# A new table of start slots and engine choices for a two-layer attention and feed-forward kernel

## The chip, the cores and the metric

The kernel runs on one core of one Trainium2 chip. The metric is the device time of one execution in microseconds (us), of which three runs of the kernel before are at hand. Engines are named as the profile names them: PE is the matrix engine, PEld its weight loads, DVE the vector engine, ACT the scalar engine, POOL GpSimd, and SP the engine that issues nearly all DMAs; SPq is SP's queue of DMA issues. The profile times one execution, instruction by instruction.

## The reference, cut to what matters

```python
x = A_x                                            # (1, 2048, 1024), bfloat16
x = x + _A_ref(_layernorm(x), A_wqkv, A_wo)        # attention, 32 heads of 32
x = x + _B_ref(_layernorm(x), B_w1, B_b1, B_w2, B_b2)
x = x + _A_ref(_layernorm(x), A_wqkv, A_wo)        # the same weights again
x = x + _B_ref(_layernorm(x), B_w1, B_b1, B_w2, B_b2)

# _A_ref: q, k, v = x @ wqkv; each token attends to W = 8 tokens, 2 apart (0, 2, ..., 14 back):
#   softmax(q . k * Dh**-0.5) over those 8, the sum of their v, then @ wo
# _B_ref: h = relu(x @ w1 + b1); (h * h) @ w2 + b2, with F = 3584
```

## The kernel before

The 2048 tokens are cut into four blocks of 512, and the two layers make eight units u = 0 to 7. A unit does layer norm and transpose of its block (SA), the q, k and v products (SQ, or SQ7 with seven block products in place of eight), the window attention on DVE (S2: products named P, sums named tree, weighted values named pr), the wo product with residual and second layer norm (SW), the first feed-forward product with its squared relu (SF1) and the second (SF2). From unit 1 on the feed-forward products, and from unit 3 on the q, k and v products, use the seven-product scheme: sums of weight blocks (tiles tv, made on DVE) are stored to DRAM once (w1s, wqs, tw) and loaded in later units like weights. Their results meet in PSUM banks X, Y and Z. A bank is drained either by ACT into a tile u or by DVE, in `hc` (line 1118, rr<-u,Y or rr<-u,Z) and `qc` (line 842); the relu and square of the feed-forward are `hr` (line 1125 on DVE, 1127 on ACT), `relu` (1166, 1169) and `sq` (1135, 1137).

Work of neighbouring units is interleaved. Weights come in tiles `w` of up to 1 MB (line 442, issued by SP; nine slots of class 8K). The layer-normed block is transposed by a DMA `lnT` (line 618, also on SP; its source is xn). In unit 0 the transposes are done on PE (pt, line 657) and drained by `ptc`.

Nothing in this order is found by the engines at run time. `Plan` builds a list of 4133 operations with their dependencies, and each engine gets its operations in one fixed order. That order, and which of two engines does an operation that may run on either, come from a table, `STARTS`:

```python
raw = zlib.decompress(base64.b85decode(STARTS))
n = len(raw) // 3
for i, o in enumerate(self.ops):
    o.num, o.prio, o.pick = i, raw[i] + 256 * raw[n + i], raw[2 * n + i]
    if o.pick:
        o.eng, o.dur, o.lat, o.fn = o.alt
```

So operation i has a start slot (16 bits, one slot is 0.02 us of the planner's own time) and one bit that picks its second engine. `run` then places the operations by these slots; sorting each engine's operations by slot gives the order in the program. The planner has its own constants for durations and transfers (a DMA lands a mean time after the queue has come to it); these are not in the table and do not change. Semaphores follow from the order: an instruction waits for what it reads, and for the last user of the buffer slot that it writes. A class of buffers hands out its slots in about the order in which their last users come in the program. Class 2K (eight slots) matters below: xt, xn, tv and rr share it, so an `hc` that opens a new rr can have to wait for the landing of a store of tv or of a transpose of xn.

Of the kernel before, what the change touches and what calls it, by code (L numbers as in the profile page):

```python
# [17 lines left out]
H = 32  # L18
W = 8
# [28 lines left out]
def _win_ap(a2d, col0, n, nw=W, wstep=-1):  # L48
# [5 lines left out]
    "c-rlF1z1(vwm)0x5Co;W6p-$cMkEvjq`SLA>F#b2rKAK2K}xzC0Rcfu6l@Hz<3HBMd*8X|o^$Sb@Bh8`?z`XptvSb-Bj%W6jJ@~TYj2DyT*Z{-<L`CdH|S+dx<2x|>r@|+O`dF>+WL5eRs5Xw<z6h#"  # L54
    "j7o={ug_hMTY2{MymF=rbSI+?$^9~9Pkw37TJ=tmOeywNEX`XQ^{N<0**_TIyHwykRQwu}@LBAIawYfjCt@}UR!nN%J0?oy4G(7C-W}SB^U^knn+xu;&mf$CR&`ZreXnWs3)%Qq(Q~{X=1#uZ@>i3u"
    "gne5)syX(o8@I3zwU4oWk5&lt#p!c%61OfZMpQ`Q-^3O<JnFN<x_3sfTr?ER<@<ojJGHQOQsb8aP2W8@MN@X9{NDt--#)!?vh%%THFxkVQ|MAaoh@D9JcgDxtN5)E+fnNw0vA%Bb~=jzBKO@3J<Oeq"
    "4ihb>NW2^-$b9p@4&%{dkdHVsp3h!T)#gi~YU(?EICf-zT;?2o)5sj2W@=|F{dpgzZ<b%=!|O<N-;K7XsJlM4$Y)oodvle<KYNf+(lE}iqJNE9;F+lU+r+zS_a)1+XwR`PXAd402pwI*p;a^Y*&XK5"
    "YAGzxZO_w4PU!IegeTUC;b|4$^!XD?oa6mN`!N+knuOKrw<EN9BM)9)e^enER9t*E5i`L<G|VbJtf6T71OK34`!s=a^?uIRZ|e#lFin%+)~;d-MLvnb#-XJd#HeNp(7sdDo?L%SQNq!@it)U>n_Iv!"
    "lX$F&)7PrEXlJM{?69|Bkc@n{s(r#R_x?imiO3bR*IgXsy5lSx0S((d=_B7&XGr6<beI`w9*)Tc*KYGyqzwMJSo~FPh$7{pf%5Ym#tgiO#yYlk7a^JsQdjTTXNSre4F^YVJ)cuFbB@m)Quc8!pwm$B"
    "3dtnLb!&e0&hw2!;TGBCw|6Xq^=E{9-cYd?()N=kch;<63NG)C$Q5~Mj7D8GOG)W+%!_SpjAiH_XYk+aU>39Mezi(OB>i-rDgV7{X*un*Yhlms_Hh=SZ=|32%~j8boX3<YJ)t-C_0%_=2$dz=yH^&Q"  # L60
    "A1{-C<Qo0>=tACoi>yP~F^A4wyJk3GZ;|!9^C`J}r7;)hXA_?#Zh^%Bje5;n6TDo{945Xzqqfe>?Ds55>oH3%7)Kf61mm21DiYLr$Z#&~!+elz%<!I4#;S|p;GSea<tLGil(-3UpXP_MYjTmQ%a(i@"
    "iQgZZh%-K>jd^-pDY$Qsg+KJXQ|;<AQDXJh+}bCrS%c4mPG_ZvNqMDXifqf<=JdW^CuU4++~hJ+y)-Nm!gq0tJ8IzDxU`>4+??J}`p8_-#z&IQ_ldM3VVH!eheiz>@HE%R)x!&iqs+Daze|#*yJk64"
    "jaQsC+zql><h_0Mz3km>r|w*{hc(Pz5>EwD7ZOMxq?D>rd3<qi?<21NuIw-0Pvl&ymoMiw@`_C{mr64D(2eJ3c4yQwQsOgm_nrD*I0X@98?4MITza>Clp<qwh9WR;ptsfa$83|&ZXs)2uU=86X(5NJ"
    "26fcB>}3Ld#|DwW<jTTj?~}B4ckn5cKD0{dr6w&tXJvXxxW($7yngiTg~=aGJ%=2znya#?UpJ8F_AKq^F5>C9-*c9`^xXY@i&Q`Bd9osdDB2C*`aM3EJc(O|_R6QcUx~A<oEUEq3`uI6_QXr;(&aMD"
    "ANz>kS@dFdN>u9k6Y7YN2AeY{EiyQ3*L`W!#y=~5RbeOU9oX9<^^Bm#o3_0WzDmfhnX@Q#ZZBb$^z>~mx!4UNuPE!6+{!u6zTURSkT>~AP}J~LKQ$aj&@?Nq=Rs7{m#KA%ZhU!On}_F!VjgRzd>ZoX"
    "Di$tEJSux_ozTnlbkh@)M_dKNl;>YwP^`YsXr8z#oA3QPeVjAA4uh~q%)MRpg>5&9W!k7!fn=p_=blXF1R-r7eGax<1i8~QPUqfF@933DM;yyMpB3VMR(pA65=)WC)*$T-XXNSLZVI;vtbn-<su6dI"
    "diFe)x^3FpVV=hGu_&`yt9Amca+fy-evd34?S4wpcOMukrSEf0<(W&xh^ybP?X`VC7~DeK^+mi(^djA8!>dCn2GexB_GI)L#mi2cQtym2>NixH%d|fV`_b7SHK@mme9>W0A`xUfrX2o+KVis1&;NSr"
    "Ol3R~0|}n0@letz_5Q3`X@vOop^caoBW$mC&Dz_29BVgiGD(E?-@2+c3RuqX5W1Vnh<<-Dy5;$VNj>$@kGFz-868K4Y}Q&GC7dYj+X$U}q>3dAqX)ZC$EtG3o?3cOI1*G;3}(ONl#jdFEA!=Oa7VeR"
    "sBhEWqv19z3Jy%iTP2Tvh+<<+Q_;J;Q0EPJ{~(qmHf3^1c91k-o7_C*3-{|P6RABc_aZIkMO2%s%IjP~&8@L3l8zZumv@4X9=GU!`-9iy@Sx{8NsH8wx<@<8(PK3C@icqrTzj9p@}Dp=2zf7J)%1na"
    "a8p!e&fsMNiAv3n1;NIcuGQm<W%(M+xUx>B*}ZM?>*5~G-`a7x=~Nas6cTqCY|9^;<XI1kTzxMc)QSH#eScd;t@;^-J%iM>Ej!(&Jtj}nj3<na#ZI~8&spTtkEzK#^l+)ce07EFZO_N7$sw~dm5PC$"  # L70
    "{rj};{V4^0DpW>q9A$7+JR6?s#9^<8<1030HMmz{NO+Ag$3IM?d9q-*OG;~)p-!W;RJ6>`c-xh}(s8>sXPMc4WUgfC%F(GvqLXc0%}nmYAG8Q4tF|xWzBKD-l4B2kX1K2S#npQPPpCrjCN-D!9kL&l"
    "0vgx#1udHfnIgT2ryrP`I_jiYKlW*-7Z?-H7`?fD(!wURQ@KoUP4_xy5}yivFs`%Ve)J||{O5)r+(y<ESj!LijIgh-|F9{;jT@Ap^lM_(p9vLQHLW!lS&+-OcrxIW*mqW{vt_gF;)|y{Vno^xIe10!"
    ">5p~nTM=WYW-L%y964%Y({RIQTaYEbL$@X!SIYa^((bNZ;p^0PvBzh*JZG423u_;}*X7BX+Q#0s4w~vJqu1LwYp~VC@j>zxgSXW6I{Mdj>ll1X@sDEWY}HYnD*=wp4O_WdpELJ{xMV7?OiX<7<-JUF"
    ")MSI0PQ8p!Uy^#NaB`Cb2j$=TNOg)Oe_14k^O#Y=h@`M|<S3CTS@>Ya9!25J?%7SM(v@b?)I0BN3U7Z;c&0Axv%f>nn<MLIUo;?|_prQvMc|oJMqC?)ex$u5Wwg`LetcD5&L39}dvm%^6H6AfP4=;r"
    "zJW)BBPE_MWR;s$d#ODp-*US4?>_QV37s25seGl=Wz^s2R%`LSU+fX2^<`S@QbR-;6}#m9Kr(}hFDyDA?gdq2TP}=XINV?|%zI;3<oIzzEaebWYUQj=MfX$wkp}-~^7e(wh5I}n!x7cZJ*|DqZ`XUe"
    "7Q^Z8Q?6K{{Aain+>S={Ea9t`+@&mhMf)&$n?<*pHvQSwh59cqE>L~bNlV-hU=`L=7K-N3m~FgoOV){#X8NrpB;=Jt`NE{#Gp>uYq;V7xFIdSVvgDmTBSqz^Nqn+P6t5_@wq#B|Nj~jM^zBY}l}Qe1"
    "hZb2MC%d5po9)X%RrOU?eLvLh&ZlKv%gvM4-w5){sx&LGX6Y!I19q3Si$qA=g2@{xh_J9_S9oG2jUBTE8qG3eMum!>?33MEiy7sY3+iFSt2`vHEky2X9V>Sm_k(!E<Ia7iKy$P4H!l4&!h`1vr81Aa"
    "aWa&e`EhMZwUXsJ!#T&>FA6Tr#nPZOg4)gw@n)I?41d5B^2>d6q>5BG%Daw5?cw!o?&|v@Hn+Jv$B6R`qzYCT-0>eNRLrxP2M-Ec-uh@UubJd|GBHr9Y-LY~{&N7E$u#z*M23XsinS8W*bzeQ-dVg2"
    "jmEc$68UYxo8P=h^l}!yT7`Y$O6G8{$2w24C^26n-NdR@LK3;dlbW)i>@~2nvP^26ajSVXrpuHNOPX&!K`?UPqT$F+{2uNV0`lj~BCa`~B@&Np@wATei=VQ-{i1YJmHb?Z;*I=_e#Tc?;}!)GB&v6g"
    "DF)qh=%JLUtabc^sgO^>mp)FguqkHexzqK*;N|7l#MJHqL@P4=79Jl&hr-u5+B^2NY$!v|jQdVuN@uy(w#yQI6YUzLO%U4Z5>k&^Raz*t#x}`!ZyMwYD^1U#aDF8xsB~uVjWq28H-9Q(W#0knvo|;_"  # L80
    "M$gMk&k<JceHU(?UC?uItX4st7&%px-YLz73eic_YiAapZRL;J622zOaYSQUNY&;_INe$Y(HE{%27cG=CL4>HqsBUdjYP+uW_+;IkV@*hVI>p(f>Whvlkh@n+c?>KA;V&3=U@SiD^n}xrBB!>QkJIt"
    "ReXZl2Yy6#;X3G_{i-Z<xywAIVVpadH}lifegmue2`@dis&^LjD^G>-CPFcIm3`yy2vJy_y{Qz@GydT7`;%!UyGa+lSR=dFj~rL(z%MQod+Bn8+eApqAz`GMTxo}b!|o=wT7yH}42kYX+Op?d0a#a>"
    "j0%V?MxC*ZG`HD5c-;IVz;5yhBmA^4nc9^P)5)oN$ueA4fe)5QY9HNtyVkrt-%Dn2!+7kIZ0OO5*Vt@_v1{H5nlF%=%{Pw>N(EMa`b3z3=kg<Y>WlhwqWYcI*KJ!zEvvU#SDqwMlN?cQxVoc%T*AZV"
    "N(UjQuT)hLj%z{c4^vO&-cbq1`g_a<&lbdUZ*E6)2sH0nIVuDS+3%qUW&CG!vnlS2xDT68Xgp#wyX~GD9Z);CnuXyzHH1TF{+hGsE9r?Bfk_zC)Q^{kE#@TIl=-SO)9l|z<#VY8zc_AP*lX6p{Z4z9"
    "g?htoZh0{_t(f(BGf|+zoX=#YlpBW8SCJv<cwEl=^HdsAkIyOvQEORLm^3|)>$z*HAGRdy5=qsBFYhLPWBc5-b@E<<PiEQM^E&tBw#zX;C`3%Zm}4&6J>hf*&!F_Mtz$rM=`7Br79yEYuH;#~sH*)f"
    "%5TDF3~HwIZ6Y+8d$ZP0Tnt_m#5i+uMEmnv<RH5#PFR0r6Tv2r4VJnhN8J&|u^8Ssmo8(CY@a^DResOqCzQ_RjnB#wUp`_n3a@yay?{DJoTkH1zgD?OZ`$G0T^389`i|M5>WNNCn?M;uc+(fjkXe$&"
    "?-mvK8Ozj0*h+7Ni{6k3NavsHA~D_}wQn*>HL7^`_H?{;MtEo6J{{A&Cg)b=6KdxVKg{1|UAtuYiR7k|b3x&9WvI~UaSETZ;+duGdAHbTxrB#D#e-GrT~b53wRml<iwDz59@9yB8K#NN)Z1PieMQ*0"
    "#}IjLxBf}{n<vs*NvFqrzmeHAWKB8LD8`kKlFQ}Xdw%K^CTR+}1(l{xbD4A5$Oqi0-W4+6{M9!sFWK0%2C?K7%@s3dHoi{NoOyl9bH4AhTZ3=mJvOVe$JBf)8`ru&$YkExOd4Fo%$nIFIYp=z?bbSL"
    "=~$deD{Jl{>YBH(QPukTwcHl-1*_zecQbgRLj^q}Lxx9eqZ+*_<%${Je9N6<xgh7^_nPv$l!6B8y1}4hY~$@mN6a$=Nd1PYZmgjA`b>DQ%O>OwZ;`#;Ta;pUy<9!CkAZ;#py?qr0eT34fpK6#8__s)"
    "81oPo7Ek~d7S`dzm@u)h0XR6gSlGC@z+ekD4n9615k3Jf9zH$+0U;qVCJrtxE|`BwaPa_W@(bYO;bCIoz&3n{NI-~B2pfq2c=!ZFM~H}y963USkHmzaghYfO13|RJ#3V3*k{pGB2I(<UQqp6`j$<4;"  # L90
    "1bJd01QP?2#=*fv=SzU(Kte)H3_*xsJM1SQJW5J(6ao?-1R)?eMnr@KVaNc-$SH8h$VkbK0gjX79zPBgKtV}%oE%mZ6cm({BqS7!OiUCE42)FN)YLRIWCz~IkCBj4P?3^SAv#)GI(k|<y5s2G<P=C0"
    "N-AnPI(jM^8cHfABn%Z56*Z!#rDI@ZVrF1uq^6;zrbb7kfdeV&=;>(?8yHz=4?stDoRSjlNkd1^0Fw?t4<M(cqhn%Xre|QFr)ObgW@bQxk&%*$>^L>qF{BFQNOW)pCMG7B%w%u~<bci<qA;I4d6ESt"
    "GcyYd3o9EtD-ZxX`w18)PH=E=a&mH=I>pHa<P<j#4=*n_FCQN>6ALpFGcyw%9WxUvGYc~dD<gmjIf8+O88mEctROH0SQr`EnAuOVo@8TVVMV~k1{xN2juRXwIS!6uXJ=w!XJO|A4c7?-kPj2n30BaY"
    ";@~=ofP;gBl@0Xl=r!bW;uQBOZf*`9-c!81VB|#dB%?&yOHPHnKIF(tK~KfN2xZZ;!wybPUOpZ^E_5wCJp5eff}kV-4}g=4hMNby<mIL3;o%0x%ge{Y#}5zy@bC-p3kU*)PC)~p1$>|cNl=)Nj~DIB"
    "$Ir)))(L__NJJQY2?_}b3keGdhzkk|3k!>gh=_|zAdm!KesnmrR#a3{Qc_$}QVOC7z!p(aF;OuwadAm0DJf}b>C*_4k(QBFI4vzBub`lysHlWYC0RK+B_$>0Gs?=!XH?FdQBgSy<Lp@>ArTQ_VNnqQ"
    "5m6Bl0Z|AKLqb$cNDK*zjtm}XK|)Mi44sptI6y*F91+DuL6ih7WCcV@5^a|}fD{ZVX@p2gNJ#^gl0;8P6G`>-X-QZdTr#H*AR{9q2@EmHfFLU)1ydFl2;}4u3+VqM$;!z91IQ`J$jQmb%PYvsD9Fnq"
    "Rm&+V!GLO&<rNeal$Fjv%?iqA6qV0F)vCNg&^i%*bVr3mp@(9^P@;qcQXk|fDXn-0I;Et71~f}W32D|@Rpqm)05uqA&WIoiL{bw|S65S4*U->7C#i7`a2}v~?mTc!O-(IT6~swJO<fIuxWiBfcQuW3"
# [1329 lines left out]
```

## Time and profile before

| | |
|---|---|
| device time, median of 3 runs | 1184.14 us (1182.77 to 1184.89) |
| the profiled execution: its own time | 1182.16 us |
| its span, first to last instruction | 1180.4 us |
| mean granted PE clock | 0.997 |
| PE busy | 1155.3 us, 7607 matmuls |
| DVE busy | 1070.6 us, 1527 instructions |
| ACT busy | 663.3 us, 1280 instructions |
| DMA | 346.54 MB, mean 294 GB/s |

The profiled execution is 1.98 us faster than the median of the three runs. PE is the engine that is nearly always busy, so what counts is where PE stands still; the idle time of the others counts only where PE waits for it. [...] a busy PE row can hide a lower clock, which is in a row of its own (PEclk).

### The profile page before, as it was taken

The page shows a single profiled execution, that of the slowest core. Times are in us where ns is not written, and L with a number is a line of the kernel's source. Part 1 is how long each engine was busy: PE and PEld are TensorE (multiplying, and loading weights), DVE is VectorE, ACT ScalarE, POOL GpSimd, SP SyncE. Part 2 cuts the span into 40 slices and gives each one's busy share as a digit, 9 for nine tenths or more (in the row PEclk, how much of TensorE's full clock was granted, in tenths as well). Part 3 has the DMA queues.
Part 4 walks back from the last instruction along what each step waited for, and adds up shares of the span by engine and source line. Part 5 has one row for each costly group of instructions (what it writes and reads, how often), then busy time and mean ns, then how long its engine had stood idle before and what let it go on. Part 6 is the DMA issues. An engine that isn't in the chain of part 4 may idle for free.

```text
span 1180.4 us, 19527 instructions
## 1 busy us (share of the span) xinstructions
PE 1155.3 (98%) x7607; PEld 741.0 (63%) x7607; DVE 1070.6 (91%) x1527; ACT 663.3 (56%) x1280; POOL 3.0 (0%) x10
## 2 busy tenths in 40 slices
PE   7999999999899999999999999999999999999998
PEld 4444444446755778467874678646885668844863
DVE  5899969999799999988999999997999999997763
ACT  6435972179731699216990578704895156824640
POOL 1000000000000000000000000000000000000000
PEclk9999999999999999999999999999999999999999
DMA  9526899999899999989999799988999889797783
GB/s 321 179 104 211 270 319 296 305 302 289 302 352 323 257 343 286 341 309 283 341 314 365 281 292 312 319 319 282 333 340 335 312 288 303 264 350 303 274 297 127
DMA packets 131325, 346.54 MB, mean 294 GB/s; under 512 B 63328, under 2 KB 71520, under 8 KB 109984
## 3 DMA queue, kind: packets, MB, share of 16 engines
q1 hardware_dynamic: 131008, 345.02, 86.2%
q8 instruction: 59, 0.97, 0.3%
q0 software_dynamic: 224, 0.28, 0.1%
q14 instruction: 34, 0.28, 0.1%
HBM read 302.26 MB, written 29.36 MB: 281 GB/s over the span
## 4 chain that ended last, share of the span: by engine, by line
PE 79%; DMA 9%; DVE 8%; ACT 2%; issue 2%; SPq 0%; DVEq 0%; ACTq 0%
PE X L1208 14%; PE X L1146 11%; PE py L1024 9%; PE pq L729 8%; PE X L851 8%; PE Z L1208 7%; PE Z L1146 6%; PE py L491 4%; PE Z L851 4%; PE Y L1208 4%; PE Y L1146 2%; PE Y L851 2%; DMA w<-in_B_w1r_dram 2%; PE lg L911 2%; DMA w<-in_A_wqr_dram 1%
## 5 line engine op out<-in xcount | busy, mean ns | idle before, releaser
L1146 PEld LDWEIGHTS <-w 128*128 128x128 f16 (+1 forms) x2544 | 249.9, 98 | 48.1 <-issue 7.0
L851 PEld LDWEIGHTS <-w 128*128 128x128 f16 (+1 forms) x1680 | 164.1, 98 | 30.4 <-DMA w<-in_A_wqr_dram 2.6
L837 ACT CAST u<-X 128x512 f16<-128x512 f32 x85 | 48.7, 583 | 218.3 <-PE X L851 218.2
L957 DVE TENSOR_TENSOR pr<-pb,v 128x2048 f16<-128x2048 f16 x128 | 152.4, 1222 | 0.1
L1146 PE MATMUL X<-T,w 128*128 128x256 f16 x1072 | 131.4, 273 | 0.6 <-DMA w<-w1s_86 0.5
L960 DVE TENSOR_TENSOR pr<-pr 128x2048 f16<-128x2048 f16 (+1 forms) x128 | 119.4, 950 | 0.0
L1024 PE MATMUL py<-w,o 128*128 128x512 bf16 x512 | 115.1, 379 | 0.0
L1114 ACT CAST u<-X 128x512 f16<-128x512 f32 x139 | 79.0, 583 | 29.9 <-PE X L1146 26.8
L729 PEld LDWEIGHTS <-w 128*128 128x128 bf16 x552 | 53.9, 98 | 63.8
L851 PE MATMUL X<-TA,w 128*128 128x256 f16 x720 | 88.7, 273 | 0.0
L1024 PEld LDWEIGHTS <-o 128*128 128x128 bf16 x512 | 50.0, 98 | 56.3
L729 PE MATMUL pq<-xnA,w 128*128 128x512 f16 x360 | 80.3, 379 | 0.0
L589 ACT ACTIVATE xn<-xm 128x1024 f16<-128x1024 f32 x32 | 33.7, 1054 | 81.1 <-DVE xm L1028 76.9
L1118 DVE TENSOR_TENSOR rr<-u,Z 128x512 f16<-128x512 f16 x98 | 65.6, 681 | 9.1 <-PE Z L1146 4.0
L1028 DVE TENSOR_TENSOR xm<-py,xt 128x512 f32<-128x512 f32 x64 | 43.2, 686 | 17.0 <-PE py L1024 16.9
L922 ACT ACTIVATE e<-lg 128x512 bf16<-128x512 f32 x64 | 35.9, 599 | 32.2 <-PE lg L911 32.0
L491 PE MATMUL py<-w,r_1327 128*128 128x512 bf16 x224 | 49.8, 379 | 0.9 <-DVE py L504 0.9
L1146 PE MATMUL X<-xnB,w 128*128 128x256 f16 x376 | 48.5, 277 | 2.1 <-DMA w<-in_B_w1r_dram 1.7
L1146 PE MATMUL Z<-T,w 128*128 128x256 f16 x336 | 44.2, 278 | 6.2 <-DVE rr L1118 3.7
L1146 PE MATMUL Z<-xnB,w 128*128 128x256 f16 x384 | 48.8, 273 | 0.0
L1146 PE MATMUL Y<-xnB,w 128*128 128x256 f16 x376 | 48.1, 273 | 0.0
L1054 PE MATMUL ph<-xnB,w 128*128 128x512 f16 x208 | 45.7, 379 | 0.0
(468 smaller groups left out, 2102.2 us busy)
## 6 DMA issues: line engine op xcount, KB each, us to landing
w<-in_B_w_dram SPq DMA_DIRECT2D x42, 896.0 KB, 6.5
w<-in_B_w1r_dram SPq DMA_DIRECT2D x33, 1024.0 KB, 7.8
w<-in_A_wqr_dram SPq DMA_DIRECT2D x20, 1024.0 KB, 7.0
w<-wqsqv SPq DMA_DIRECT2D x20, 1024.0 KB, 7.0
w<-in_A_wqkv_dram SPq DMA_DIRECT2D x16, 1024.0 KB, 8.4
w<-in_A_wo_dram SPq DMA_DIRECT2D x16, 1024.0 KB, 6.5
w<-in_B_w_dram SPq DMA_DIRECT2D x28, 512.0 KB, 6.7
w<-tw_79 SPq DMA_DIRECT2D x14, 896.0 KB, 6.8
```

What stands on the lines that cost most here:

```text
L491: nc.tensor.matmul(bank[:], r2[:, k2 * h + j0 + j, tl * 128:(tl + 1) * 128], w[:, k2, n2, j, :], start=False, stop=(j0 + n == h and k2 == ...
L729: nc.tensor.matmul(pq[:], wv(w, c0, kd), xnT[:, :, kd, :], start=(kd == 0), stop=(kd == KD - 1))
L837: p.add("ACT", act(512), lambda: nc.scalar.copy(us[i][:], X[:]), [(X, 0)], [(us[i], 0)], UCOPY, name="u", alt=("DVE", dve(512, False), lam ...
L851: nc.tensor.matmul(bank[:, a, :], w[:, wi, k, a * 128:(a + 1) * 128], rhs(k), start=(start and k == 0 and a == 0), stop=(k == 3), skip_gro ...
L957: nc.vector.tensor_tensor(pr[:, i], pb[:], _win_ap(v[:, c + i, :], HALO + hb * HB, HB), ALU.mult)
L960: nc.vector.tensor_tensor(pr[:, :, 0:n], pr[:, :, 0:n], pr[:, :, n:2 * n], ALU.add)
L1024: nc.tensor.matmul(py[:], o[:, c, tl * 128:(tl + 1) * 128], wos[c // 4][:].rearrange("p (a b) n -> p a (b n)", a=4)[:, c % 4, sl], start=( ...
L1054: nc.tensor.matmul(ph[:], w[:, m, kd, a * 128:(a + 1) * 128], xnT[:, :, kd, :], start=(kd == 0), stop=(kd == KD - 1))
L1114: p.add("ACT", act(512), lambda: nc.scalar.copy(us[i][:], X[:]), [(X, 0)], [(us[i], 0)], UCOPY, name="u", alt=("DVE", dve(512, False), lam ...
L1118: p.add("DVE", dve(512, False), lambda: nc.vector.tensor_tensor(r[:, :, m, :], us[i][:], bank[:], ALU.add), [(us[i], 0), (bank, 0)], [(r, ...
L1146: nc.tensor.matmul(bank[:, a, :], w[:, wi, k, a * 128:(a + 1) * 128], rhs(k), start=(start and k == 0 and a == 0), stop=(k == 3), skip_gro ...
L1208: nc.tensor.matmul(banks[q][:], left(jj, q), w[:, j, :], start=(start and jj == 0), stop=(jj == h - 1), skip_group_check=True)
```

## The change

The only thing that changes is the text of `STARTS`. No operation, dependency, buffer, constant or line of code changes. Its author's words for it are: order of operations and engine choices annealed with transfers of random lateness (three draws) in place of the mean time of each.

```diff
 STARTS = (
-    "c-rlF1z1(vwm)0x5Co;W6p-$cMkEvjq`SLA>F#b2rKAK2K}xzC0Rcfu6l@Hz<3HBMd*8X|o^$Sb@Bh8`?z`XptvSb-Bj%W6jJ@~TYj2DyT*Z{-<L`CdH|S+dx<2x|>r@|+O`dF>+WL5eRs5Xw<z6h#"
...
-    "Fa"
+    "c-rlG1zgu#(l>vlL%O?50qGP35fJG=DM(2w0us^)(p}PxlyrB8bR!4|2#O*GHY)0S&QI^|z5CqHvv=Qj_uczEpZ)&N%$b=pGiPT0iDH!Fo{3+f{Gji$$;4;YeQ@%F{GDS8ag(i6+Xu%uq%<%2^kJYK"
...
+    "rT%{a9Bv!r"
 )
```

Decoded and sorted by slot, the two tables differ as follows. Of 1125 PE operations (one is up to 8 matmuls) 807 get another place, 1.9 places away on average and 37 at most. On DVE and ACT most operations move by some four places. On SP 199 of 568 DMAs move, most of them by one to three places. The engine bit flips for 127 operations:

| operation | ACT to DVE | DVE to ACT |
|---|---|---|
| u (drain of X) | 15 | 5 |
| cast | 5 | 5 |
| hr | 16 | 30 |
| relu | 7 | 11 |
| sq | 13 | 5 |
| seed | 4 | 4 |
| ln3 | 2 | 3 |
| ptc | 0 | 2 |

Three groups of moves are spoken of later. At the start of the program SP issues the four x tiles first, then the first two parts of the k weights, then three tiles xt with one of the larger k parts between them, and the other larger part last; before, the first k part comes ahead of the third and fourth x tile, and the second behind a larger part. Around 690 us of the trace a transpose `lnT` of xnB comes ahead of the load of w1r that it follows before. And around 315 us the products into Z for two feed-forward steps change places.

## The prediction, made before the change was run

> **What bounds the kernel now.** I read the page first. Its first row leaves little to win: PE is busy 98% of the span.
>
> ```profile
> PE 1155.3 (98%) x7607; PEld 741.0 (63%) x7607; DVE 1070.6 (91%) x1527; ACT 663.3 (56%) x1280; POOL 3.0 (0%) x10
> ```
>
> The work of PE is the same after the change. From the chain, 24 matmuls of 512 columns take 5.18 us (0.216 each), and 16 of 256 columns take 1.75 us (0.109); with the counts 3006, 4504 and 96 (128 columns, 0.054) that is 1145 us. So only where PE stands still, or runs at a lower clock, can anything be won. The waits of PE, longest first:
>
> ```profile
> engine line waited for: us in total, times, longest us
> PE pk L1294 <- POOL grp L387: 4.3, 1, 4.3
> PE Z L1146 <- DVE rr L1118: 3.7, 1, 3.7
> PE pt L657 <- DVE xn L639: 2.2, 1, 2.2
> PE Z L1146 <- DVE T L550: 1.8, 1, 1.8
> PE X L1146 <- DMA w<-in_B_w1r_dram: 1.7, 2, 1.4
> PE Y L851 <- DMA w<-in_A_wqr_dram: 1.2, 1, 1.2
> PE py L491 <- DVE py L504: 0.9, 1, 0.9
> ...
> PE X L1208 <- ACT X L503: 0.8, 1, 0.8
> ...
> PE X L1146 <- DMA w<-w1s_86: 0.5, 1, 0.5
> ```
>
> They sum to about 21 us, of which 7.5 lie in the first 15 us. Stage by stage, the losses are all in the first 855 us; the rows also show where the clock was halved:
>
> ```profile
> 311.00:314.30 3.30, 0.00 (x0) 0.00 (x0) 0.36 (x1) 0.00 (x0) 0.00 (x0) 1.00 1.04 420
> 314.30:317.70 3.40, 3.01 (x15) 2.15 (x15) 3.33 (x8) 1.53 (x2) 0.00 (x0) 0.50 0.58 234
> 710.30:713.70 3.40, 3.40 (x18) 2.41 (x17) 3.40 (x8) 2.40 (x6) 0.00 (x0) 0.50 1.05 422
> 855.00:1160.00 305.00, 305.00 (x2150) 208.74 (x2148) 273.63 (x406) 161.69 (x303) 0.00 (x0) 1.00 0.85 307
> ```
>
> From 855 to 1160 us PE is busy without a gap: nothing to win there. Each half-clock stretch costs about 1.4 us (15 matmuls in 3.01 us in place of 15 x 0.109; 18 in 3.40). The chain of waits tells what stands ahead of the gaps, and nearly always it is a transfer:
>
> ```profile
> 303.37 10.48 DMA wqsqv<-tv
> ...
> 540.11 11.21 DMA w<-in_A_wqr_dram
> ...
> 697.52 12.21 DMA w<-in_B_w1r_dram
> ```
>
> The median load of w took 7.0 us from issue to landing, and a tenth of them over 9.3: the waits come from the late ones. That is what the new table is said to guard against.
>
> **The change part by part.** Engine choices first. By the group rows, what comes to DVE (u and cast 0.69, sq 0.68 or 0.42, hr 0.28 or 0.35, relu 0.48, ln3 0.72) less what leaves it is +4.1 us of 1070; ACT gets -1.4 of 663. In the stretch where DVE is full (320 to 440 us, over 39.5 of each 40 us) it is about -1; 2.9 of the 4.1 fall into the last 100 us, where DVE is busy 27 us of each 40. I cost the choices at nothing: DVE's idle time covers them. Were that cover gone, they'd cost at most those 4.1 us.
>
> For the loads I counted, in both orders, the PE work that lies between the place of the issue and the place of the first product that reads it (the lead, with 0.216 us for a 512-column matmul). Before, 17 of 308 loads landed less than 0.3 us ahead of their use. Where such a load got a longer lead, its wait shrinks by the difference; I take that the transfer itself takes as long as before.
> - 298.8 us, w1s_86: lead 5.2 to 6.0, wait 0.5: -0.5.
> - 506.5, wqr: lead 4.5 to 7.5, gap 0.4: -0.4.
> - 551.4, wqr: lead 8.6 to 9.5, wait 1.2: -0.9.
> - 709.8, w1r: lead 8.6 to 10.4, wait 1.4: -1.4, and with it the half clock behind it, -1.4.
> - 777.7, w2: lead 4.5 to 7.5: -0.4.
> - 571.9, w1r: lead 10.4 to 10.4: its 0.3 stays.
>
> Two waits come from 2K slots. At 747.5 an `hc` waits 2.2 us for a transpose (DVE rr <- DMA xnA<-xn), which ends in PE's 0.8 us for the seed of X. In the new order the slot's last user is a square, not the transpose: -0.8. At 173.9 a DVE seed comes late behind stores of tv (DVE waits 5.2 + 3.5 us for them between 160 and 180); the new order gives these slots 5 to 10 us since the store's issue, before 5 to 6: -0.9.
>
> The largest wait mostly stays. At 313.9 the `hc` has stood 5.98 us for the store of wqsqv, whose slot its rr takes over, and PE for the `hc`. The new order keeps that pairing; the `hc` stands 5.8 slot-us behind the store's issue, before 4.8, but on PE the Z product behind it is swapped with the next, so PE comes to it 7.8 behind the issue, before 7.7. The three 1 MB loads ahead of the store on SP stay there. Value -0.3; bounds 0 and -5.1 (wait and half clock gone). PE's 1.8 us at 430.6 waits for a T on a full DVE, with no transfer ahead of it: 0.
>
> Sum of gains: 0.5+0.4+0.9+2.8+0.4+0.8+0.9+0.3 = 7.0 us.
>
> Half-clock rows, for the 1.4 us at 710: the trace shows 3.41 us of half clock right behind a gap of 3.7 us, and as much again behind 0.4, 0.35 and 1.43 us within 4 us. [...] by the trace smaller gaps do it too, [...] I count the one at 710. The measured rows decide: 7.0.
>
> Costs. At the start, the four x land earlier, but the last k part now has two xt tiles (0.26 MB each) ahead of it; before, those landed at 15.4 and 16.0 us behind it, it at 14.7. So it lands at about 16.0. The product that needs it started at 14.74; one of 0.88 us now runs ahead of it, so what follows starts at 16.9 in place of 16.50: +0.4 (bounds -0.9, the earlier x, and +1.3). The `ptc` that goes to ACT (1.0 us in place of 0.68) is hidden beneath that landing; without it, it would be 0.3.
>
> Ten loads get a shorter lead than their slack allows: w2 at 497.0 (slack 0.57, lead 6.0 to 4.5), wqr or w1r at 560 (2.1; 9.5 to 6.9) and at 699.1 (0.05; 6.0 to 4.3), and seven smaller ones. Together 5.0 us if each wait came in full. The 1.7 at 699 lies ahead of PE's waits for DVE and ACT at 705 to 708 (0.4 and 0.35 by the timeline), which shrink by as much as PE is later: 0.9. Of the rest (3.3) I take 1.3, since a wait gives slack to what follows. Bounds 0 and 5.0; value 2.2. Nothing on DVE or ACT is costed beyond this: an engine's place in the queue moved by some four operations, half a us each, both ways.
>
> Sum: -7.0 + 0.4 + 2.2 = -4.4. The profiled execution took 1182.16 us (span 1180.4 and 1.8 around it), so 1177.8 on its own scale. The median of the runs is 1.98 higher: 1179.7.
>
> **The rivals.** (1) All late transfers are taken care of, the one at 314 too: 4.7 us more (1.4 of them half clock), and the new shortages don't show (+2.2): -11.3, about 1173. For it: the order was sought under late transfers. Against: the pairing at 314 is still there.
>
> (2) No change. In the stretches that wait, the DMA share is 0.9 to 1.05, so a load issued earlier may only stand longer in the queue: the 10.48 us store moved 0.26 MB behind 3 MB. If half of the 7.0 is lost so, and the shortages cost 3: about -0.1, 1184. Against: the median load took 7.0 and half of them landed more than 4.8 us ahead of their use, so the queue is not full throughout.
>
> (3) Slower: the transpose at 690. SP issues in order, and a `lnT` can hold SP for long:
>
> ```profile
> 691.42 0.33 SPq L442 DMA_DIRECT2D w<-in_B_w1r_dram  x1
> 691.88 1.24 SPq L618 DMA_TRANSPOSE xnB<-xn  x1
> ...
> 699.11 5.44 SPq L618 DMA_TRANSPOSE xnB<-xn  x1
> ```
>
> The first two rows change places. If that transpose holds SP for 5.44 us in place of 1.24, the load comes 4.2 later, PE waits that much more, the half clock at 710 stays (1.4) and another comes (1.4): -4.4 + 7.0 = +2.6, about 1186.7. It decides from some 5.2 us of issue on (below that it's within 0.2%). Against: 1.24 in this trace.
>
> (4) The table doesn't act, since the planner departs from it. In the trace all four engines follow the old table's sort, so I give this no chance of its own.
>
> **How the numbers follow.** Forecast 0.60, (1) 0.18, (2) 0.14, (3) 0.08. A measurement of this kernel can tell about 0.2%, 2.4 us, from no change. Forecast: its own unknowns run from -9.1 (half of what is at stake at 314, and no shortages) to -0.7 (shortages and start in full), so 1175.0 to 1183.4; a part of it, about 0.04, is within 2.4 us. With half of (1) below, and all of (3) and a third of (2) above, the range 1173.5 to 1184.5 leaves out about 0.09 below and 0.11 above. Faster by over 0.2%: 0.56 + 0.18 + 0.03 of (2) = 0.77; within 0.2%: 0.04 + 0.11 + 0.02 of (3) = 0.17; slower 0.06.
>
> **What would show it.** In the profile after: no PE wait for w1r at about 710 and none for w2 at about 777, wqr at 551 under 0.5; the seed of X not waited for at 750; one half-clock stretch instead of two; still a PE wait of about 3.5 us for an `hc` near 315; new waits of under 1 us near 497 and 560, and of up to 1.7 near 694 to 699; `pqk` at about 16.9. Wrong if the wait at 315 is gone, if the sum of PE waits falls by less than 2 us, or if a stretch after 855 us gets gaps, since I give those no cost.

## The result, and the profile after

The changed kernel takes 1176.84 us (median of four runs, 1176.09 to 1179.14), beside 1183.45 us for four runs of the kernel before (1181.02 to 1184.89). The ratio of the two is 0.9949, with a 95% interval of 0.9927 to 0.9972. That is 6.0 us less by the ratio, 6.6 by the medians; the forecast said 4.4 less. The profiled execution took 1176.09 us, with a span of 1174.4, against 1182.16 and 1180.4.

The first row of the page, after: PE's busy time falls by 1.6 us, though its work is the same. A matmul at half clock counts as busy for about twice as long (at the start of after, eight products took 1.68 us at half clock and 0.87 at full), so this fits one half-clock stretch less.

```profile
PE 1153.7 (98%) x7607; PEld 740.7 (63%) x7607; DVE 1073.4 (91%) x1524; ACT 660.3 (56%) x1283; POOL 3.0 (0%) x10
```

The waits of PE, after (engine, line, what was waited for: us in total, times, longest):

```profile
engine line waited for: us in total, times, longest us
PE pk L1294 <- POOL grp L387: 4.3, 1, 4.3
PE Z L1146 <- DVE rr L1118: 3.3, 1, 3.3
PE pq L733 <- DMA w<-in_A_wqkv_dram: 2.8, 1, 2.8
PE X L1146 <- DVE v L842: 2.1, 1, 2.1
PE Z L851 <- DVE v L842: 1.1, 2, 0.6
PE Z L1146 <- DVE T L550: 1.1, 2, 0.6
PE Z L1208 <- DMA w<-in_B_w_dram: 0.8, 1, 0.8
PE X L1146 <- ACT e L922: 0.5, 1, 0.5
PE Y L1146 <- DMA w<-in_B_w1r_dram: 0.3, 1, 0.3
```

All gaps of PE over 0.1 us together are 17.1 us, before 21.5. The rows for wqr at 506 and 551, w1r at 572 and 710, w1s at 299 and the seed of X at 750 are gone. What transfers still cost is the start (2.8 in place of 0.8), one w2 load at 493 (0.8) and one w1r load at 697 (0.3), besides the store that the `hc` at 315 waits for. The wait for `hc` at 315 is nearly what it was (3.3 against 3.7).

The windows around the gaps show the granted clock (from:to and length in us; busy us and instructions of PE, PEld, DVE, ACT, POOL; PE clock; DMA share; GB/s):

```profile
12.45:15.86 3.41, 0.82 (x8) 0.49 (x5) 1.22 (x2) 3.35 (x7) 0.00 (x0) 1.00 1.04 425
15.86:19.27 3.41, 3.23 (x12) 1.79 (x13) 0.00 (x0) 2.61 (x8) 0.00 (x0) 0.50 1.01 420
312.80:316.20 3.40, 1.51 (x14) 1.35 (x14) 2.21 (x3) 0.00 (x0) 0.00 (x0) 1.00 1.02 420
316.20:319.60 3.40, 3.26 (x31) 2.77 (x30) 3.37 (x7) 2.57 (x6) 0.00 (x0) 1.00 0.09 28
709.60:713.00 3.40, 3.40 (x34) 3.05 (x32) 3.33 (x5) 3.04 (x7) 0.00 (x0) 1.00 1.02 352
855.00:1160.00 305.00, 305.00 (x2120) 205.81 (x2118) 269.06 (x399) 153.28 (x292) 0.00 (x0) 1.00 0.83 299
```

Both half-clock stretches of before (314 and 710) are gone, and a new one stands at 15.9, behind the wait at the start. From 855 to 1160 PE is busy without a gap, as before.

Setting the two traces side by side at equal PE work gives the difference step by step (us, after minus before; the small rest of the steps is +0.3):

| where | forecast's term | two traces |
|---|---|---|
| start, to 20 us | +0.4 | +2.0 |
| 119 to 123 | 0 | -0.2 |
| 174, seed behind stores of tv | -0.9 | -1.0 |
| 299, w1s_86 | -0.5 | -0.4 |
| 303, an `lg` | 0 | +0.3 |
| 314, `hc` behind the store | -0.3 | -1.7 |
| 430, T | 0 | -0.3 |
| 493, w2, new | up to +0.9 | +0.95 |
| 506 and 551, wqr | -1.3 | -2.0 |
| 572, w1r | 0 | -0.5 |
| 690 to 710, w1r | -1.9 | -1.2 |
| 750, seed of X | -0.8 | -1.4 |
| 777, w2 | -0.4 | -0.5 |
| 854 | 0 | -0.4 |

This table is of one execution each. How far it can be trusted is taken up below, under "stage by stage".

### The profile page after: what moved, and what is told of

Its sections match the earlier page's. It is cut to its first block, busy times and chain, and to the rows that moved or that the text cites. A ratio compares the mean times of both kernels' runs of the same rounds, so it can differ in the third digit from the quotient of the medians.

```text
span 1174.4 us, 19519 instructions
## 1 busy us (share of the span) xinstructions
PE 1153.7 (98%) x7607; PEld 740.7 (63%) x7607; DVE 1073.4 (91%) x1524; ACT 660.3 (56%) x1283; POOL 3.0 (0%) x10
## 4 chain that ended last, share of the span: by engine, by line
PE 57%; DVE 5%; ACT 2%; DMA 1%; issue 1%; DVEq 0%
PE X L1208 12%; PE X L1146 10%; PE X L851 6%; PE Z L1208 6%; PE py L1024 6%; PE Z L1146 6%; PE Y L1208 3%; PE Z L851 3%; PE Y L1146 2%; PE Y L851 2%; PE lg L911 1%; DVE v L842 1%; DMA w<-in_B_w_dram 1%; ACT u L1114 0%; DVE T L550 0%
## 5 line engine op out<-in xcount | busy, mean ns | idle before, releaser
L837 ACT CAST u<-X 128x512 f16<-128x512 f32 x81 | 46.8, 583 | 212.1 <-PE X L851 210.6
L960 DVE TENSOR_TENSOR pr<-pr 128x1024 f16<-128x1024 f16 (+1 forms) x128 | 120.3, 953 | 0.0
L1114 ACT CAST u<-X 128x512 f16<-128x512 f32 x133 | 74.6, 582 | 20.9 <-PE X L1146 18.5
L1127 ACT ACTIVATE rr<-rr,b1T 128x256 f16<-128x256 f16 (+1 forms) x85 | 46.0, 565 | 12.8 <-DVE rr L1118 12.5
```

The costliest lines, as they stand in the source:

```text
L837: p.add("ACT", act(512), lambda: nc.scalar.copy(us[i][:], X[:]), [(X, 0)], [(us[i], 0)], UCOPY, name="u", alt=("DVE", dve(512, False), lam ...
L960: nc.vector.tensor_tensor(pr[:, :, 0:n], pr[:, :, 0:n], pr[:, :, n:2 * n], ALU.add)
L1114: p.add("ACT", act(512), lambda: nc.scalar.copy(us[i][:], X[:]), [(X, 0)], [(us[i], 0)], UCOPY, name="u", alt=("DVE", dve(512, False), lam ...
L1127: alt=("ACT", 0.11 + len(ms) * 0.23, lambda: nc.scalar.activation(out=v(), in_=v(), func=ACTF.Relu, bias=self.b1T[:, f:f + 1], scale=1.0)))
```

## Experiments: the engine choices

The kernels of all experiments emit an order that is worked out beforehand and given as a plain sort, so that one part can be changed and every other operation stay in its place. The edit that all share (line numbers in their profiles are about 20 lower than in the two kernels compared above: 1126 for 1146, 1098 for 1118, and so on):

```diff
     def run(self):
+
+        return sorted(self.ops, key=lambda o: o.prio), None
+
+    def run_planner(self):
```

The ratios below are to the kernel before, run beside each of them on the same chip.

**New order, old choices.**

```diff
-o.pick from the new table (127 operations differ)
+o.pick from the old table; order on each engine by the new slots
```

> After's order with before's 127 engine choices: an operation that changes its engine keeps its slot, now in the other engine's queue. Prediction's view: the choices are hidden by idle time on DVE and ACT, so within 1 us of after, 1176 to 1178. Rival: in an order as tight as this the choices are part of what makes it fit, and single operations come too late on the engine that they go back to: some us slower, up to 1185, spread over many small waits of PE for DVE or ACT.

It took 1181.99 us (14 runs, 1179.96 to 1184.64), ratio 0.9995 (0.9983 to 1.0007): no gain at all. Some of the waits of PE that are not in the list of after:

```profile
PE Z L1126 <- DVE rr L1098: 3.5, 3, 2.6
PE X L1126 <- ACT u L1094: 1.7, 3, 0.7
PE lg L891 <- ACT rr L1146: 1.0, 2, 0.6
PE lg L891 <- DVE rr L1098: 0.6, 1, 0.6
PE X L1188 <- DVE xm L1194: 0.4, 1, 0.4
PE Y L1126 <- DVE rr L1098: 0.2, 1, 0.2
```

Ten such waits, of 0.17 to 0.80 us each, lie between 303 and 1031 us, three of them in the stretch behind 855 us that was free of gaps; together they are 4.7 us, and the profiled execution is 5.1 us longer than that of after. (The first row also holds the wait at 314, here 2.6 us.) No one wait carries it. Nearly all are drains (u or rr) done a little too late for the PE operation that needs them. One reading stays open: an operation that changes its engine keeps its slot, in a queue that was laid out without it, so any other 127 flips might have cost as much. No run tries that.

**Old order, new choices,** the fourth corner.

```diff
-o.pick from the old table (127 operations differ)
+o.pick from the new table; order on each engine by the old slots
```

> Order of before (by its slots, on every engine), engine choices of after: the fourth corner beside before, after and the run with the new order and the old choices (which was within 0.1% of before). If order and choices are worth something each by itself, the choices win here what their loss cost there, about 5 us: 1178 us against a before of 1183. If the choices only fit the order that they were annealed with (their moved operations are queued at the places that the new order left for them), it is no faster than before: 1183 to 1188, with new waits of PE for an rr, u or v of under 1 us each in place of the transfers' waits, which all stay (314, 551, 710, 777). The prediction's own term (choices cost and win nothing) would say 1183.

It took 1188.3 us (1186.84 to 1189.69), ratio 1.0037 (1.0025 to 1.005): slower. Its gaps over 0.1 us sum to 29.1 us, against 21.5 before. The transfers' waits stay, and others come beside them:

```profile
PE X L1127 <- DMA w<-in_B_w1r_dram: 3.9, 3, 1.9
PE Z L1127 <- DVE rr L1099: 3.8, 2, 3.5
PE Z L1189 <- DVE xm L1195: 1.7, 1, 1.7
PE Y L1127 <- ACT xnB L641: 1.6, 1, 1.6
PE X L1127 <- ACT u L1095: 1.1, 3, 0.6
PE X L1189 <- DMA w<-in_B_w_dram: 1.0, 1, 1.0
```

The four corners, in per cent of before: both old 0; new order alone -0.05; new choices alone +0.37; both -0.51. So neither part has a worth of its own. The old choices lose what the new order wins, and the new choices are harmful in the old order: each set of choices fits only the order with which it was found.

## Experiments: SP's order against the others'

**Order of SP new, all else old.**

```diff
-order of SP by the old slots
+order of SP by the new slots, carried to the old order's time at equal PE work
```

> Before's order and engine choices on PE, DVE and ACT, after's order on SP. Theory A: the order in which SP issues the DMAs makes the longer leads; then most of the 8 us won in mid-stream comes with it, about 1177 us. Theory B: PE's order does (it frees the slots of w for the next load and says when a load is read), and SP's order only matters at the start and for the load of w2 at 777; then no gain but that 0.5, and at the start a loss, since the product that needs the last k part runs first and waits until 16.0 us in place of 14.7, with a half clock behind it: about 1185, with the waits for wqr at 551 and w1r at 710 still there.

It took 1208.34 us (1206.35 to 1210), ratio 1.0203 (1.0189 to 1.0218), far from every number expected. The timelines of SP's queue and of PE near the end (start, length, engine, line, operation; in brackets the idle time before):

```profile
1145.28 15.59 SPq L422 DMA_DIRECT2D w<-tw  x6
1178.89 0.34 SPq L422 DMA_DIRECT2D out_dram<-xo  x1
1179.33 0.87 SPq L422 DMA_DIRECT2D w<-in_B_w_dram  x2
...
1184.60 3.15 PE L1188 MATMUL Z<-w,r 128*128 128x512 bf16 x7 [5.95 <-DMA w<-in_B_w_dram]
```

SP issues in order. The store of an xo is ahead of two loads of w2 and waits for an xo that DVE, in its old place, makes late; the queue stands 17.9 us, and PE 5.95 us for a load whose data had been ready in DRAM all along.

**Order of SP old, all else new,** the mirror.

```diff
-order of SP by the new slots
+order of SP by the old slots, carried to the new order's time at equal PE work
```

> After's order and engine choices on PE, DVE and ACT, before's order on SP: the mirror of the run above. Theory A: most of the gain is gone, about 1182. Theory B: the gain stays, less 0.5 at 777 and plus the 2.0 that the start lost: about 1175.5, with no PE wait for a load at 551 and 710.

1196.22 us (1191.7 to 1198.38), ratio 1.0102 (1.0085 to 1.0118): slower too. Two waits for w2 (5.3 us) head the new ones, and between 123 and 181 us PE waits three times for DVE or ACT (7.6 us), with two half-clock stretches behind (mean clock 0.997). Both mixes bring waits that neither whole has, so they don't tell what one order is worth by itself. So the gain can't be put down to the order of the loads or to that of the engines; each mix is worse than either whole.

## Experiments: stage by stage

**The middle alone.** The forecast counts 1.3 us of gain at 506 and 551 us; the two traces show 1.9 at 551 and 572. This is the old order and choices, but with the new ones for the 417 operations placed from 510 to 612 us of the written-out order.

```diff
-old slots and picks throughout
+new slots and picks where 510 us <= old slot < 612 us
```

> Before, with after's order and choices only for the 417 operations that before places from 510 to 612 slot-us. By the traces after won 1.4 us at 551 (wait for wqr) and 0.5 at 572 (w1r) here. If the longer lead of those loads in this stretch is the cause, 1.9 faster than before, 1181.5, with both waits gone in the profile and the others of before unchanged; if it needs what came ahead of it in the program (DVE's and the DMA queue's state), no change, with the waits still there.

1182.12 us (14 runs, 1177.82 to 1187.39), ratio 0.9998 (0.9986 to 1.0011). In its profile the stretch is mended:

```profile
540.00:600.00 60.00, 59.85 (x546) 53.21 (x545) 59.12 (x85) 52.92 (x104) 0.00 (x0) 1.00 1.09 332
```

PE is busy in 59.85 of the 60 us; the waits of 1.24 at 551 and 0.28 at 572 are gone, and this execution took 1180.09 us, 2.1 less than the profiled one of before. The median shows none of it: its interval leaves room for 1.7 us at most. Why it doesn't follow is not shown. Single executions differ by more than that: the 31 of the kernel before that stand beside it scatter from 1179.4 to 1186.8 us, more than any single term of the sum.

The traces of the other experiments hold more draws of the same stretches. The gaps of PE over 0.1 us, summed:

| from, to (us) | old table there: before, the same move in before, new then old | new table there: after, start undone, store first, both moves, old then new |
|---|---|---|
| 484 to 578 | 1.86, 1.95, 1.78 | 0.77, 0.44, 0.80, 1.00, 0.84 |
| 690 to 716 | 2.19, 1.82, 1.83 | 2.55, 2.46, 2.54, 2.72, 2.71 |
| 725 to 785 | 1.29, 1.67, 1.12 | 0 in all five |

The sums are steadier than their parts. With the old table the load at 551 made PE wait 1.24, 0.96 and 0 us in these three executions, and the one at 506 0.33, 0.51 and 1.48: a single wait of 1 us is a draw, and what one load doesn't cost, its neighbour does. By the sums the new table wins about 1 us in the first of these stretches and 1.4 in the third, and loses 0.6 in the second.

**Old up to 280 us, new behind it; and the mirror.**

```diff
-one table throughout
+old slots and picks before 280 us, new ones from there (and the mirror)
```

> Order and engine choices of before for everything placed before 280 us of the written-out order, those of after from there on. By the comparison of the two profiled executions, after loses 2.0 us at the start, wins 1.2 us of it back by 175 us, and all the rest of its gain (5.4 us) lies beyond 280 us. If gains by stage add up, this kernel is without the loss at the start: 1182.9 - 5.4 = 1177.5 us against a before of 1182.9, so about 0.7 us slower than after or equal to it. If one profiled execution is a poor guide to where the gain lies (as with the middle alone, which showed its two waits gone and no gain), it can lie anywhere between before and after, above 1180 us. The third view, that old choices and new order only fit together as a whole, would have a new wait of several us at the seam, over 1184 us.

> The mirror: order and engine choices of after before 280 us, those of before from there on. If gains by stage add up: +2.0 at the start and -1.2 by 175 us make +0.8 us on before, about 1183.7 us; if the gain is spread over the whole and one profile is a poor guide, between after and before, about 1180 us; a seam that doesn't fit gives over 1186 us.

Old then new: 1178.59 us (1177.4 to 1180.28), ratio 0.9962 (0.9948 to 0.9977). New then old: 1181.63 (14 runs, 1178.62 to 1185.62), ratio 0.9989 (0.9977 to 1.0001). The two sum to 0.0049 below one, about the whole gain of 0.0051. So on stretches this long the gain may well add up, with 4.5 us beyond 280 us and about 1.3 before, though each ratio is known to 0.0012 to 0.0015 only, and the second can't be told from one. The table of the two traces put 5.4 us beyond 280 and +0.8 before it. The first falls 0.9 us short of that, and a new wait at the seam (1.9 us for an rr at 291 us, not in before or after) is enough to make it up. The second has the other sign, within its noise. With the same start as after, this execution waited 1.8 us at 15.1 and no half clock followed. Of the four kernels here with that start and a profile (after, the old choices, this one, and the store first, below), two show a half clock at 16 us (0.50 from 15.86 and 0.51 from 15.96, behind waits of 2.77 and 2.10 us) and two don't (waits of 2.42 and 1.8): the +2.0 at the start is in part a draw.

**The start undone.**

```diff
 # SP, first eleven DMAs (x: the blocks; k0 to k3: parts of the k weights; xt: tiles)
-x x x x k0 k1 xt k3 xt xt k2
+x x k0 x x k3 xt k1 k2 xt xt
```

> After, with the first eleven DMAs on SP in before's order, all else as in after. By the traces the start lost 2.0 us: a wait of 2.8 us for the last k part at 16.0 and the half clock behind it, against 0.8 and no half clock before. If SP's order is the cause, the k part lands at 14.7, the wait shrinks to under 1 us, no half clock follows: 1.6 to 2.0 us faster than after, about 1175. If the ptc that went to ACT is what holds the start (the rival), less than 0.5 is won, since the next product still waits for it until about 16.9.

1175.53 us (1173.24 to 1177.04), ratio 0.9927 (0.9914 to 0.994), beside 0.9949 for after; the intervals overlap. In its profile the wait for the k part at 16 us and the half clock behind it are gone, and the start is 2.6 us shorter than in after. Of this 1.1 us come back at 427 us, where a half clock appears that after doesn't have.

**The last store first.** The wait at 314: the `hc` needs the slot of a tile tv whose store stands on SP behind three loads of w, up to 1 MB each, in the old order and in the new.

```diff
 # SP, around 301 us
-lnT xnA; w; w; w; wqsqv<-tv; xt
+lnT xnA; w; wqsqv<-tv; w; w; xt
```

> After, with one DMA moved: the last store of wqsqv before 315 us is issued ahead of the second and third of the three 1 MB loads that it stood behind. Theory: the hc at 313.9 waits for the landing of that store, whose 2K slot it takes, and PE waits for the hc; the store then lands at about 308.5, ahead of the hc's turn at 310, DVE's 4.1 us and PE's 3.3 us are gone, and the wait for DVE at 427 shrinks too, as DVE is full from there on: 3.3 to 4.1 us faster than after, about 1173. Rival: the landing of other DMAs of that burst is what ends the wait (they land between 310.7 and 314.5), and the wait stays: no change against after, 1176.8.

1171.9 us (1171.56 to 1173.34), ratio 0.9902 (0.9889 to 0.9916): 4.9 us below after by the medians, 5.6 by the ratios, with one DMA moved by two places; 3.3 to 4.1 were expected. The waits of PE in its profile: the row for rr, 3.3 us in after, is gone.

```profile
PE pk L1274 <- POOL grp L367: 4.3, 1, 4.3
PE pq L713 <- DMA w<-in_A_wqkv_dram: 2.1, 1, 2.1
PE X L1126 <- DVE v L822: 2.1, 1, 2.1
PE Z L1126 <- DVE T L530: 1.1, 2, 0.6
PE Z L831 <- DVE v L822: 0.8, 2, 0.6
PE Z L1188 <- DMA w<-in_B_w_dram: 0.8, 1, 0.8
```

The rows of the store's tile tell why. They are for the last three such stores, first for after, then for this kernel (issue to landing in us, least, median, longest; the longest is this store):

```profile
DMA to landing us min/median/max: 4.2/4.3/9.8
```

```profile
DMA to landing us min/median/max: 4.1/4.1/6.1
```

Issued 1.9 us earlier and landing in 6.1 us in place of 9.8, it is there some 5 us earlier, and the `hc` no longer waits for it (in after, DVE waited 4.1 us).

**The same move in the kernel before.**

```diff
 # SP, around 301 us, in the old order
-w; w; wqsqv<-tv
+wqsqv<-tv; w; w
```

> Before, with only that store moved ahead of the two loads. Before lost 3.7 us of waiting and 1.4 of half clock there, so 5.1 faster than before, about 1178, if the store is the cause in both kernels; no change if the wait has another cause in before. It also says how much of the gain of the whole new table one moved DMA is worth.

1177.69 us (10 runs, 1175.49 to 1181.34), ratio 0.9958 (0.9942 to 0.9974). One DMA moved in the old order is worth 5 us, nearly as much as the whole new table (6.0). The mean clock was 1.000 in nine of the ten executions and 0.999 in the tenth (0.997 in the profiled one of before), so the half clocks are gone too. The profile is of the slowest of the ten (1181.34 us) and shows less of the gain: the store comes later in it, at 306.2, takes 8.2 us to land, and DVE still waits 2.5 us for it. PE's waits between 308 and 324 us fall from 3.72 to 1.29, of which 0.86 is for a load of w1s.

**Both moves in the new order.**

```diff
-x x x x k0 k1 xt k3 xt xt k2
+x x k0 x x k3 xt k1 k2 xt xt
 ...
-w; w; wqsqv<-tv
+wqsqv<-tv; w; w
```

> After, with both changes that helped: the start's DMAs in before's order and the store of wqsqv ahead of two loads. If the two gains (1.3 and 4.9 us against after) are independent, 1170.6. If the half clock only moves from the start to another gap (the run with the start alone showed one at 427 us that after did not have), the start's gain is lost again in part: 1171 to 1172.

1171.39 us (1169.83 to 1172.82), ratio 0.9906 (0.989 to 0.9923). The start's gain does not add to the store's: the wait at 15 is gone, but the clock is halved at 422, as the second expectation had it. This is the lowest median of all the kernels, not to be told apart from that with the store alone.

## Why the prediction was right, and where it was wrong

The direction is right, and the time lies within the range: 1179.7 forecast, 1176.84 measured. The sum behind it is less right than its result. (A count in it is off by one, 3007 matmuls of 512 columns and not 3006; its 1145 us stand.)

- **Leads against late loads: right in kind.** Every load that the forecast named as winning (299, 506, 551, 710, 777) lost its wait, and the two that hang on a 2K slot (174, 750) shrank or went. The gains at 551 (-1.4) and 750 (-1.4) were about half a us larger than counted. The one at 572, given nothing since its lead is unchanged, went as well: it is 0.28 to 0.48 us in three traces with the old table there, and in none of those with the new one. "Sum of PE waits falls by 2 us or more" holds: 4.4.
- **New shortages: right at the first, too high in sum.** The w2 load at 493 waits 0.8 us and costs 0.95, its full shortage of 0.93. The one at 699 waits 0.3 (forecast: up to 1.7), and no other of the ten shows. Forecast 2.2, found about 1.2.
- **690 to 710: the overlap was wrong, and luck hid it.** The load's wait (1.4) and the half clock (1.4) are gone as forecast. In their place PE waits 0.55, 0.60, 0.47 and 0.64 us for a v, a v, an e and a T between 702 and 709, where it waited 0.40 and 0.35 before. The forecast had these waits for DVE and ACT shrink by 0.9; they grew, and the stretch as a whole waits longer in all five traces with the new table there (2.5 to 2.7 us, against 1.8 to 2.2). The -1.2 of the two traces is the half clock, which of the four traces with the old table there (the middle alone is the fourth) only that of before has.
- **314: the wait as forecast, the clock not.** The wait is 3.28 in place of 3.72 us (forecast -0.3). The half clock behind it is gone, -1.4 more. "One half-clock stretch instead of two" came true, but the one that stays was to be this one and is that at the start. The stretches together were forecast at -1.4 and came to -1.2, by luck.
- **The start: the landing as forecast, the clock not.** The last k part landed at 16.0 us, as worked out, and eight products at full clock would have put what follows at 16.9, as forecast. It started at 17.7, because the clock was halved from 15.86 to 19.27: +2.0 in place of +0.4. The mis-sized term is this half clock, 1.6 us. As the mirror run shows, the clock isn't halved there in every execution.
- **The engine choices at nothing: the step that failed.** "DVE's idle time covers them" argues from the busy share of long stretches, and PE's waits came from the place of single drains in a queue. With the old choices the new order wins nothing (0.9995), with the new choices the old order loses 0.37%. Order and choices hold the gain only together; without the new choices it is lost in waits of 0.2 to 0.8 us for single drains. The forecast's gains were read off the order of the loads alone, and the total came near the truth because the choices came along with it.
- **The rivals.** The transpose at 688 held SP for 1.24 us, as its old one did, so the third rival had no cause. The second, no change (1184), lies outside the interval. The first, with all late transfers taken care of, was said to fail at 314: it did, and with that store moved the kernel takes 1171.9 us, near the 1173 that the rival stood for.

Why the table doesn't mend 314 is not shown. A reading of the code, untried, is this: the planner's list of free slots gives that `hc` the slot of an earlier square in its own model, while in the emitted program it takes the tile of the late store. A search over the planner's times wouldn't see the stall.

## What to carry to other kernels

Read a single wait of about 1 us in a profile, and a half clock behind it, as one draw; sum the waits over a stretch, over several executions if you can, and test a mended stretch by its median before counting on it. An order and its engine choices are one object: cost them together, and don't mix queues of two orders. Where PE waits for a drain that waits for a store, look at what stands ahead of the store in its queue: moving one DMA two places won nearly what a new order of 4133 operations did.

## What the runs showed of the hardware

A run is seen here in its one profiled execution. In before from 314.33 to 317.74 and from 710.28 to 713.69 us, and in after from 15.86 to 19.27, the granted clock was 0.50; in the 3.41 us ahead of each of these stretches and in the 3.41 us behind it, it was 1.00. In the run with SP's order new the slow products at the start lasted longer: from 15.67 us on 16 matmuls of 256 columns took 3.60 us and the eight of 512 columns behind them 2.98, beside 1.92 and 1.89 in before.

Gaps that look alike were followed by different clocks. A gap of 2.1 us for a v near 425 us stands in the run with the start undone, the run with both moves and the run with the store first, here in rows of 3.41 us; in the first two the second row begins with the half clock:

```profile
423.79:427.20 3.41, 1.34 (x14) 1.20 (x13) 3.41 (x5) 3.31 (x8) 0.00 (x0) 1.00 1.19 338
427.20:430.61 3.41, 3.33 (x18) 2.07 (x16) 3.41 (x6) 3.35 (x8) 0.00 (x0) 0.50 0.96 396
```

```profile
418.99:422.40 3.41, 1.35 (x13) 0.99 (x12) 3.41 (x5) 3.25 (x9) 0.00 (x0) 1.00 1.19 267
422.40:425.81 3.41, 3.41 (x18) 2.46 (x17) 3.41 (x7) 3.35 (x6) 0.00 (x0) 0.50 0.97 401
```

```profile
418.72:422.13 3.41, 2.49 (x20) 1.66 (x18) 3.38 (x4) 3.34 (x7) 0.00 (x0) 1.00 1.16 307
422.13:425.54 3.41, 1.91 (x16) 1.50 (x16) 3.41 (x7) 3.31 (x8) 0.00 (x0) 1.00 1.07 385
425.54:428.95 3.41, 3.26 (x30) 2.96 (x31) 3.41 (x6) 3.31 (x9) 0.00 (x0) 1.00 0.98 406
```

In the first two PE is busy 1.34 and 1.35 of the 3.41 us ahead, and the next row runs at 0.50. In the third the gap is spread over two rows (2.49 and 1.91), and the clock stays at 1.00. In after the same gap (2.07 us) left PE busy 1.34 of the 3.41 us from 425.42, as in the first two, and the clock was 1.00 there and in the next 3.41 us. Its gap of 3.28 us at 314 (1.51 us busy of the 3.40 from 312.80) was followed by 1.00 too; the shorter 2.77 at the start, with 0.82 busy of the 3.41 from 12.45, by 0.50. In before, 1.62 busy of the 3.41 us ahead of 710.28 was followed by 0.50. So neither the length of the gap nor the busy time ahead settles in these traces whether the clock is halved, and what settles it is not shown.

A half clock behind a gap is therefore treated here as a draw. The start shows it: the wait of 2.10 us in the run with the store first is followed by a half clock, and the longer one of 2.42 in the run with the old choices isn't. The mean clock shows it too. By an estimate, one stretch lowers it by 0.0014 (half of the measured 3.41 us in 1180), and of 31 executions of the kernel before 13 have 0.997, 9 have 0.998, 7 have 0.999 and 2 have 1.000: about two stretches in the first, none in the last. Their median times are 1183.46 us for the first and 1180.09 for the last.
